# Sketched attention with a mixture of experts behind it on one core: a listed order for the first batch and a moved router placing

## The chip, the cores and the metric

One Trainium2 chip, one of its cores. The metric is device time in microseconds (us) of one execution of the kernel, median of several runs. The core has five engines that run beside each other[...]: TensorE (PE; its weight loads are shown as PEld), VectorE (DVE), ScalarE (ACT), GpSimd (POOL) and SyncE (SP), and 16 DMA engines that move data on request of SyncE, ScalarE or GpSimd.

## The reference

Inputs: q, k, v of shape (4, 4, 1088, 32), two sketches S1 and S2 of shape (8, 32), eight expert embeddings of 128, a temperature tau, w1 (8, 128, 1024) and w2 (8, 1024, 128), all float32. Output: (4352, 128).

```python
def phi(x):                      # 64 features of a row of 32
    a = np.einsum('rd,bhsd->bhsr', S1, x)
    b = np.einsum('rd,bhsd->bhsr', S2, x)
    return np.einsum('bhsi,bhsj->bhsij', a, b).reshape(*x.shape[:-1], r * r)
q_p, k_p = phi(q), phi(k)
kv = np.einsum('bhsf,bhsd->bhfd', k_p, v)
z = np.sum(k_p, axis=2)
x = num / den                    # q_p @ kv, over q_p @ z + 1e-6; heads side by side: (4352, 128)
logits = (x / |x|) @ (emb / |emb|).T / tau
expert_idx = np.argmax(logits, axis=1)
gate_w = softmax(logits)[expert_idx]
out[mask] = gate_w[mask, None] * (np.maximum(x[mask] @ w1[e], 0.0) @ w2[e])   # for each expert e
```

## The kernel before

The tokens are handled as two halves, m = 0 and m = 1 (two of the four batches each, 17 tiles of 128 tokens). The diff's words "first batch" and "second batch" mean these halves. Tiles go in groups of four (GROUPS: tiles 0 to 3, 4 to 7, 8 to 11, 12 to 15) and a single rest tile, called "r". For each group there are steps, small functions that issue instructions on several engines:

- `ktr`, `qtr`: four transposes on TensorE into a small PSUM bank ("t", two buffers) and a ScalarE copy (`turned`, L372 to L377). In the steps of the first half a 0 is added to the name (`ktr0 1`).
- `kab`, `qab`: the sketches of the group on TensorE (L392, L394), into a bank that the list names ("ab", "acc" or "t"). `kb`, `qb`: ScalarE copies of them (L400, or L405 where both factors are copied, `both_factors`). `kp`, `qp`: products of the two factors to 64 features (`features`, L410), on VectorE, for most key groups of the second half on GpSimd.
- For queries of the first half, features are made in turned form: `pairs` (32 matmuls into two pairs of big banks, L558), `sec` (ScalarE copies, L567), `prod` (VectorE products into the tile "held", L570).
- `kv` (L472): keys times values, summed over all tiles of the half in one bank ("acc"). `total`, `trkv`, `kvT`, `kve`, `kz`: the sum is copied and multiplied with the embeddings into the tile "kz".
- `trqp`, `qpT`: query features transposed (L588) and copied (L594 or L597). TWO_BANKS says for which groups the transposes go to the banks acc and ab instead of a pair of big banks. `nd` (L610): features times kz, into a pair of big banks. `x` (L623 to L630, VectorE): the attention rows (tile "xg") and their logits ("lg").
- The router (L680 on): `best`, `pick` (maximum and one-hot, VectorE), `place` (small matmuls that count each token's place within its expert, L702 to L706), `take`, `split`, `mark` (VectorE). `write` stores rows and logits to the DRAM tensor "rows" (SyncE, L732, L736). In the second half, the router works on two parts: tiles 0 to 7, then 8 to 16.
- The tables: the first half alone fills EARLY = 10 blocks of 128 tokens that belong to one expert each; `count`, `rest`, `find`, `exp0`, `sums` (L799, L801), `tokens` (L816) and `others` make the early table: which tokens lie in a block ("dst_i") and which expert it has ("exp_i"; exp_0 for the first block). A late table for the remaining blocks is made the same way when the second half has been routed, on ticks 13 to 17.

Then follow 36 blocks of the mixture of experts (MoE). For block i: `fetch` (an indirect gather of 128 rows on GpSimd's queue, L929), `turn` (a transpose into a bank "t", L935, and a copy xTb by ScalarE or VectorE, L937), `weights` (512 KB of w1 of the block's expert, issued by SyncE, which first reads the expert's number, L941, L946), `up` (16 matmuls into a pair of big banks, L983, and a ReLU on ScalarE, L991), `norm`, `inverse`, `shares`, `share` (the gate, ScalarE, GpSimd and VectorE), `down` (16 matmuls, L1019, alternately into acc and ab, then a scaled copy and an indirect scatter on GpSimd's queue, L1031).

What sets the order: every engine works off its instructions in the order in which they are emitted. `put_at(tick)(after, rank, f)` puts a step f on a tick with a rank; `emit` goes through the ticks, and within a tick by rank. Ticks below 4 hold the first half, tick 4 the long list ORDER, tick 10 + i block i of the MoE: second layer's address 29.9, up 30, turn of the next block 45, share 73, down of the block before 74, weights two blocks ahead 79. AFTER_UP stands at rank 30.5 and AFTER_TURN at rank 46 of tick 10. In the first half each step has a rank of its own in `keys`, `queries` and at the end (`put(0, 49.8, ab)` and so on), so that, within a stage, ScalarE copies `sec 0`, kT of the next group, `sec 1`, qT of the next group. The big banks are two pairs, handed out in turn: a new user of a pair waits until the one before it has been read.

In the list before, the step order behind the sums is: tokens, qp r, qp 3, qp 2 on VectorE, with the first gather (`fetch0`) after tokens. The router's first placing of the second half sits on tick 11 at rank 70.5, ahead of down(0) at 74, in a spare part of the big pair of `nd 1 3`.

Of the kernel before, what the change touches and what calls it, by code (L numbers as in the profile page):

```python
# [27 lines left out]
NC = S // HALF  # L28
# [9 lines left out]
SPAN = NC - 8  # L38
WIDE = SPAN + SPAN % 2
NEXT = 172  # L40
TWO_BANKS = (1, 2, 3)
NCP = 8 + WIDE
ROW = DM + E
COLS = D + 1 + E
# [21 lines left out]
def kernel(  # L66
# [284 lines left out]
    TABLE1 = 12  # L351


    ORDER = """
tremb; total0; ktr 1; trkv0; kvT0; kab 0 ab; kb 0; trqp0r; kve0; kab 1 acc; kz0; ktr 2; nd 0 0; kb 1; ktr 3;
kp 0; nd 0 1; kab 3 ab; kb 3; x 0 0; nd 0 2; kab 2 t; x 0 1; kp 1; x 0 2; kb 2; kp 3; kv 0; nd 0 3; ktr r;
qtr 0; kab r ab; kp 2; kb r; kv 1; x 0 3; qtr 1; qab 0 ab; best 0; qtr r; qb 0; kv 2; qtr 3; qp 0; place 0;
count; kv 3; kp r; take 0; kv r; total; qtr 2; qab 1 t; trqp 0; split 0; rest; trkv; qab 2 acc; find; kvT;
mark 01; mark 00; qab 3 ab; exp0; qb 1; qb 2; kve; qpT 0; qab r ab; qp 1; qb r; sums; tokens; qp r; qb 3; kz;
trqp 1; qp 3; fetch0; qp 2; qpT 1; nd 1 0; trqp 3; qpT 3; nd 1 1; fetch 1; turn 0; x 1 0; trqp 2; qpT 2;  # L360
norm 0
"""
    AFTER_UP = "others; x 1 1"
    AFTER_TURN = "nd 1 2; trqp r; qpT r; nd 1 3; x 1 2; x 1 3"
    steps = {}

    def turned(tiles, rest, n, tag):
# [66 lines left out]
        for bank in ("ab", "acc", "t"):  # L434
            steps[f"{name} {bank}"] = lambda bank=bank: f(bank)

    def keys(m, c0, c1, put=None):
        n = c1 - c0
        s = {}

        def tr():
            s["kT"] = turned(None if n == 1 else k_sb[m][:, :, c0:c0 + 4], k_rest[m], n, "kT")

        def ab(bank=None):
            s["ab"] = sketch(ab_bank(put.tick, n, 1) if put else ab_next("k", n, bank), s["kT"], n)

        both = m == 1
        by_pool = m == 1 and c0 > 0

        def b():  # L450
            if both:
                s["ab"] = both_factors(s["ab"], n)
                s["b"] = s["ab"][:, :, 1]
            else:
                s["b"] = second(s["ab"], n, "kb")

        def prod():
            s["kp"] = features(s["ab"], s["b"], n, "kp", nc.gpsimd if by_pool else nc.vector)

        def kv():  # L460

            if c0 == 0:
                acc[m] = ps_one("acc")[:, :8 * D].rearrange("p (i a n) -> p i a n", i=2, a=2)
            for c in range(c0, c1):
                rest = c == NC - 1
                for i in range(2) if rest else (c // NK,):
                    for p in range(2):
                        for u in range(2):
                            h = 2 * p + u
                            vo = v_rest[m][i][:, h] if rest else v_sb[m][:, h, c]  # L470
                            to_ones = (H - h) * D if rest else ((H - h) * 2 * NK - c) * D
                            nc.tensor.matmul(  # L472
                                acc[m][u * HALF:(u + 1) * HALF, i, p], s["kp"][:, c - c0, h],
                                bass.AP(tensor=vo.tensor, offset=vo.offset,
                                        ap=[list(vo.ap[0]), [to_ones, 2], [1, D]]),
                                start=p == 0 and c == 0, stop=rest, skip_group_check=True)

        def total():
            s["kv"] = work.tile([P, 2, 2, D], F32, tag="kv", bufs=1, name="kv")
            nc.scalar.copy(s["kv"], acc[m][:, :, :, :D])  # L480
            for u in range(2):
                r = slice(u * HALF, (u + 1) * HALF)
                nc.scalar.copy(kz[m][r, :, :, u, :D + 1], acc[m][r, :, :, :D + 1])

        def tr_kv():
            s["t"] = ps_small()[:, :P]
            nc.tensor.transpose(s["t"], s["kv"].rearrange("p i a d -> p (i a d)"), ident)

        def kvT():
            s["kvT"] = work.tile([P, P], F32, tag="kvT", bufs=1, name="kvT")  # L490
            nc.scalar.copy(s["kvT"], s["t"])

        def kve(stage):
            if stage == 0:
                s["kve"] = ps_small()[:, :P // 2]
                nc.tensor.matmul(s["kve"], s["kvT"], en_blk.rearrange("p a u e -> p (a u e)"), start=True, stop=True)
                return
            ps = s["kve"].rearrange("p (i a u e) -> p i a u e", i=2, a=2, u=2)
            for u in range(2):
                r = slice(u * HALF, (u + 1) * HALF)  # L500
                nc.scalar.copy(kz[m][r, :, :, u, D + 1:], ps[r, :, :, u])
        if m == 1:
            g = name_of(c0)
            steps.update({f"ktr {g}": tr, f"kb {g}": b, f"kp {g}": prod, f"kv {g}": kv})
            by_bank(f"kab {g}", ab)
            if n == 1:
                steps.update({"total": total, "trkv": tr_kv, "kvT": kvT, "kve": lambda: kve(0), "kz": lambda: kve(1)})
            return
        put(-1, 50.6 if n > 1 else 55.5, tr)
        put(0, 49.8, ab)  # L510
        put(0, 49.85, b)
        put(0, 53, prod)
        first = c0 >= NC - 5
        put(*((2, 51) if c0 == 0 else (1, 47) if first else (1, 55)), kv)
        if c1 == NC:
            steps.update({"total0": total, "trkv0": tr_kv, "kvT0": kvT, "kve0": lambda: kve(0), "kz0": lambda: kve(1)})

    xg, lg, spare, turned_q = {}, {}, {}, {}

    def queries(m, c0, c1, put=None):  # L520
        n = c1 - c0
        w = n * P
        s = {}
# [9 lines left out]
            s["qT"] = turned(None if n == 1 else q_sb[m][:, :, c0:c0 + 4], q_rest[m], n, "qT")  # L533

        def ab(bank=None):
            s["ab"] = sketch(ab_bank(put.tick, n, 0) if put else ab_next("q", n, bank), s["qT"], n)

        both = m == 1

        def b():  # L540
            if both:
# [91 lines left out]
        if n > 1:  # L633
            steps.update({f"nd {m} {step}": nd, f"x {m} {step}": x})
        if m == 0:
            put(-1, 53 if n > 1 else 55.6, tr)
            if n == 1:
                put(0, 50, ab)
                put(0, 50.5, b)
                put(0, 54, prod)  # L640
                steps.update({"trqp0r": tr_qp, "qpT0r": qpT})
            else:
                put(0, 50, pairs)
                for j in range(2):
                    put(0, 50.5 + 0.2 * j, lambda j=j: seconds(j))
                    put(0, 54, lambda j=j: prods(j))
        else:
            steps.update({f"qtr {step}": tr, f"qb {step}": b, f"qp {step}": prod,
                          f"trqp {step}": tr_qp, f"qpT {step}": qpT})
            by_bank(f"qab {step}", ab)  # L650
        if c1 == s1:

            bank = (lambda: spare[m]) if m == 0 or c1 < NC else (lambda: table_bank[0][:, 0])
            best, pick, place, take, split, mark, write = router(m, s0, s1, g, bank)

            if m == 0:
                steps.update({"best 0": best, "pick 0": pick, "place 0": place, "take 0": take, "split 0": split,
                              "mark 00": lambda: mark(0, NK), "mark 01": lambda: mark(NK, NC), "write 0": write})
            elif c1 < NC:
                at_rank = {best: (10, 72), pick: (10, 72), write: (10, 90), place: (11, 70.5),  # L660
                           take: (11, 71.2), split: (13, 76.5), mark: (14, 76)}
            else:
                at_rank = {best: (12, 31), pick: (12, 31), place: (13, 31), take: (13, 32), split: (13, 32),
                           write: (12, 90), mark: (16, 32)}
                put_at(13)(0, 30.9, lambda: table_bank.append(ps_big()))
# [381 lines left out]
    for i, group in enumerate(GROUPS):  # L1047
        for tiles in group:
            for m in range(NM):
                keys(m, *tiles, put_at(i) if m == 0 else None)  # L1050
                queries(m, *tiles, put_at(i) if m == 0 else None)
    put_at(-1)(0, 40, more_constants)
    put_at(-1)(0, 52.9, turn_sketches)
    put_at(1)(0, 55, iotas)
    put_at(2)(0, 60, norm_emb)
    put_at(3)(0, 51, scale_emb)
    put_at(3)(0, 52, steps["ktr 0"])
    put_at(1)(0, 91, lambda: clear(0))
    put_at(2)(0, 91, lambda: clear(1))

    count, rest, others = plan_early()
    find, high, low, sums, tokens, *_ = table(0, 1, lambda: early["key"])
# [12 lines left out]
    for i, name in enumerate(x.strip() for x in ORDER.split(";")):  # L1075
        put_at(4)(0, 47.2 + 0.01 * i, steps[name])
    for at_, names in ((30.5, AFTER_UP), (46, AFTER_TURN)):
        for i, name in enumerate(x.strip() for x in names.split(";")):
            put_at(first)(0, at_ + 0.01 * i, steps[name])
    put_at(first)(0, 32, lambda: weights(1))  # L1080

# [9 lines left out]
    put(3, 73.5, find)  # L1091
    put(3, 76, high)
    put(4, 74, low)
    put(5, 31, sums)
    put(5, 31.1, lambda: tokens(0, PAIRS))
    put(5, 45.1, first_rows)
    put(5, 75.1, halves)
    put(5, 75.2, lambda: tokens(PAIRS, LATE))
    known = table1 + 5 - first
    put(5, 31.2, lambda: [fetch(i) for i in range(EARLY, known + AHEAD + 1)])  # L1100

    def in_ticks(b0, b1, tick):
        for i in range(b0, b1 + 1):
# [79 lines left out]
```

## Time and profile before

| What | Value |
|---|---|
| median of 3 runs | 207.26 us (206.97 to 208.28) |
| the profiled execution | 206.99 us |
| its span (first to last instruction) | 205.2 us |
| TensorE busy, weight loads busy | 194.0 us, 183.3 us |
| VectorE, ScalarE, GpSimd busy | 87.8, 103.0, 106.8 us |
| first transpose of the MoE (L935) starts | 55.10 us |
| up(0), up(1), up(2) start | 56.30, 61.36, 67.27 us |
| DMA moved | 39.42 MB, 192 GB/s in the mean |

How to read it: times in a profile count from the start of the span. The page's slices show the busy share of 40 equal parts in tenths. A timeline line gives start, duration, engine, source line, operation, output tile <- input tiles, shape and count; brackets give the idle time of that engine just before and what ended it. A line of the waits reads: engine, tile and line that waited, <- who released it, then total us, times and the longest. "Issue" means that nothing in the profile explains the wait.

### The profile page before, as it was taken

Reading aid. Unit: us, or ns where it says so; the run is one execution under the profiler, and the core shown is the slowest. Engines: PE = TensorE matmul, PEld = TensorE weight load, DVE = VectorE, ACT = ScalarE, POOL = GpSimd, SP = SyncE. Lnnn points to the kernel's source line nnn. Section 1 sums busy time; section 2 is a strip of 40 time slices with the busy share of each in tenths; the row PEclk is TensorE's granted clock in tenths of the full one; section 3 lists DMA queues with packets and bytes.
Section 4 is the critical chain, followed back from the end, with each engine's and each line's share of the span. In section 5 each row is a group of like instructions: output and inputs, shape, how many; then the busy total and the mean of one; then the engine's idle time right before and its main releaser. Section 6 shows DMA issues by size and latency. Waiting matters only on the chain.

```text
span 205.2 us, 6948 instructions
## 1 busy us (share of the span) xinstructions
PE 194.0 (95%) x2586; PEld 183.3 (89%) x2586; DVE 87.8 (43%) x378; ACT 103.0 (50%) x294; POOL 106.8 (52%) x137
## 2 busy tenths in 40 slices
PE   7989998999897999999999999999999999998991
PEld 7658788798787999999999999999999999997891
DVE  6577847788948368931221312212122122122100
ACT  2656461436373546534654555546555465776330
POOL 4010035302743567666777767677676776753033
PEclk9999999999999999999999999999999999999999
DMA  4999899568354996645465665665656794592000
GB/s 132 334 274 315 179 311 292 165 221 248 70 216 136 318 341 175 184 155 154 146 199 177 165 210 156 181 196 154 210 161 176 229 313 152 200 268 114 3 26 24
DMA packets 28162, 39.42 MB, mean 192 GB/s; under 512 B 5738, under 2 KB 21366, under 8 KB 28130
## 3 DMA queue, kind: packets, MB, share of 16 engines
q1 hardware_dynamic: 25776, 34.23, 56.7%
q0 software_dynamic: 2304, 4.74, 7.6%
q8 instruction: 22, 0.36, 0.7%
q14 instruction: 10, 0.08, 0.1%
q10 hardware_dynamic: 50, 0.01, 0.0%
HBM read 34.37 MB, written 4.73 MB: 191 GB/s over the span
## 4 chain that ended last, share of the span: by engine, by line
PE 88%; DVE 3%; ACT 2%; DMA 2%; issue 2%; POOL 0%; POOLq 0%; DVEq 0%
PE ps_big L983 27%; PE ps_acc L1019 14%; PE ps_ab L1019 14%; PE ps_acc L472 4%; PE ps_big L610 4%; PE ps_big L988 4%; PE ps_t L375 4%; DMA xs<-rows,dst_i 2%; PE ps_t L935 2%; PE ps_big L558 2%; PE ps_acc L1022 2%; PE ps_ab L1022 2%; PE ps_t L801 2%; PE ps_acc L105 1%; PE ps_ab L394 1%
## 5 line engine op out<-in xcount | busy, mean ns | idle before, releaser
L983 PE MATMUL ps_big<-xTb,wb 128*128 128x128 f32 x512 | 62.8, 276 | 0.0
L1031 POOL DMA_INDIRECT out_dram<-y,dst_i x36 | 37.5, 1043 | 44.4 <-ACT sq L996 20.1
L983 PEld LDWEIGHTS ps_big<-xTb,wb 128*128 128x128 f32 x512 | 59.7, 192 | 0.5 <-issue 0.2
L991 ACT ACTIVATE hT<-ps_big 128x1024 f32<-128x1024 f32 x36 | 36.8, 1024 | 37.2 <-PE ps_big L983 36.4
L929 POOL DMA_INDIRECT xs<-rows,dst_i x36 | 37.6, 1043 | 18.9 <-DVE dst_i L816 10.9
L937 DVE COPY xTb<-ps_t 128x128 f32<-128x128 f32 x29 | 8.4, 291 | 61.9 <-PE ps_t L935 61.9
L1019 PE MATMUL ps_acc<-w_sb,hT 128*128 x256 | 31.3, 275 | 0.1
L1019 PE MATMUL ps_ab<-w_sb,hT 128*128 x256 | 31.2, 275 | 0.0
L1019 PEld LDWEIGHTS ps_acc<-w_sb,hT 128*128 128x128 f32 x256 | 29.9, 192 | 0.1
L1019 PEld LDWEIGHTS ps_ab<-w_sb,hT 128*128 128x128 f32 x256 | 29.9, 192 | 0.0
L997 POOL TENSOR_TENSOR norm<-norm,half_c 128x1 f32<-128x1 f32 x36 | 21.3, 595 | 3.6 <-ACT sq L996 3.0
L1010 DVE TENSOR_SCALAR gate<-gate 128x1 f32<-128x1 f32 x36 | 5.5, 152 | 22.1 <-ACT probs L1007 22.0
L1028 ACT ACTIVATE y<-ps_acc,gate 128x128 f32<-128x128 f32 x18 | 6.6, 367 | 14.3 <-PE ps_acc L1019 10.9
L410 POOL TENSOR_TENSOR kp<-both 128x1024 f32<-128x1024 f32 (+1 forms) x4 | 6.5, 1619 | 11.8 <-ACT both L405 10.8
L1028 ACT ACTIVATE y<-ps_ab,gate 128x128 f32<-128x128 f32 x17 | 6.2, 367 | 10.3 <-PE ps_ab L1019 8.7
L996 ACT ACTIVATE sq<-xs 128x128 f32<-128x128 f32 x36 | 10.9, 302 | 1.0 <-DMA xs<-rows,dst_i 0.9
L1007 ACT ACTIVATE probs<-xs,norm 128x8 f32<-128x8 f32 x36 | 10.6, 295 | 1.3 <-DVE norm L1001 1.3
L935 PE MATMUL ps_t<-ident,xs 128*128 128x128 f32 x36 | 10.2, 282 | 0.9 <-DMA xs<-rows,dst_i 0.9
L472 PE MATMUL ps_acc<-v,kp 128*64 128x64 f32 x256 | 9.4, 225 | 0.7 <-issue 0.5
L472 PEld LDWEIGHTS ps_acc<-v,kp 128*64 128x64 f32 x256 | 8.3, 138 | 1.6 <-issue 1.2
L377 ACT COPY kT<-ps_t 128x512 f32<-128x512 f32 (+1 forms) x10 | 5.2, 524 | 7.6 <-PE ps_t L372 3.8
L988 PE MATMUL ps_big<-xTb,wb 128*64 128x64 f32 x128 | 7.8, 223 | 0.0
(246 smaller groups left out, 291.2 us busy)
## 6 DMA issues: line engine op xcount, KB each, us to landing
wb<-in_moe_w_dram SPq DMA_DIRECT2D x36, 512.0 KB, 4.8
w_sb<-in_moe_w_dram SPq DMA_DIRECT2D x16, 256.0 KB, 4.8
rows<-xg SPq DMA_DIRECT2D x4, 544.0 KB
v<-in_v_dram SPq DMA_DIRECT2D x4, 512.0 KB
v<-in_moe_w_dram SPq DMA_DIRECT2D x4, 512.0 KB
k<-in_k_dram SPq DMA_DIRECT2D x3, 512.0 KB
q<-in_q_dram SPq DMA_DIRECT2D x3, 512.0 KB
xs<-rows,dst_i POOLq DMA_INDIRECT x36, 3.5
```

The costliest lines, as they stand in the source:

```text
L472: nc.tensor.matmul(acc[m][u * HALF:(u + 1) * HALF, i, p], s["kp"][:, c - c0, h], bass.AP(tensor=vo.tensor, offset=vo.offset, ap=[list(vo.a ...
L929: nc.gpsimd.indirect_dma_start(out=xs[i][:], out_offset=None, in_=rows[:2 * S if t == 0 else N + 1], in_offset=bass.IndirectOffsetOnAxis(a ...
L935: nc.tensor.transpose(ps[:, :P], xs[i][:, :DM], ident)
L983: nc.tensor.matmul(ps[:, u, j * P:(j + 1) * P], w[:, f * P:(f + 1) * P], x, start=True, stop=True)
L988: nc.tensor.matmul(ps[r, u, j * P + b * HALF:j * P + (b + 1) * HALF], wh[:, f * P + c * HALF:f * P + (c + 1) * HALF], x[:, b * HALF:(b + 1 ...
L991: nc.scalar.activation(hT[i], ps, ACT.Relu)
L996: nc.scalar.activation(sq, xs[i][:, :DM], ACT.Square, accum_out=norms[i])
L997: nc.gpsimd.tensor_tensor(out=norms[i], in0=norms[i], in1=half_c, op=ALU.pow)
L1007: nc.scalar.activation(p, xs[i][:, DM:], ACT.Exp, scale=norms.pop(i)[:, 0:1], accum_out=gate[i])
L1019: nc.tensor.matmul(ps, h[:, f * P:(f + 1) * P], ws[0][:, f], start=f == 0, stop=f == NF - 1)
L1028: nc.scalar.activation(y, ps, ACT.Copy, scale=gate.pop(i)[:, 0:1])
L1031: d = nc.gpsimd.indirect_dma_start(out=out[:, :], out_offset=bass.IndirectOffsetOnAxis(ap=dst_i[t][:, j:j + 1], axis=0), in_=y[:], in_offs ...
```

## The change

The first half's steps get names and an order of their own in a list HEAD, all at tick 0; ranks in `keys`, `queries` and at the end are gone. Within a stage, both `sec` copies now come before the copies of the next group, `kv0 1` comes behind the last `pairs`, and `iotas` and `scale emb` behind the rest tile. ORDER is rewritten; AFTER_UP becomes empty, with `others` and `x 1 1` moved into ORDER. Behind the sums VectorE's order is now qp 1, tokens, qp 3, qp 2, x 1 0, qp r, others, x 1 1; `fetch0` and the three further gathers stand next to each other. Query group 3 of the second half is no longer copied with both factors: its product reads one factor from PSUM. Group 1 leaves TWO_BANKS. The first placing of the second half takes a small bank and moves to tick 12 at 31.5, its take to 12 at 44, the write of the rows to tick 11 at 80. In the late table, sums and what follows (tokens, first_rows, two gathers) move from rank 31 to ranks 74.1 to 74.4 of tick 17, behind a down layer, and halves with its tokens to tick 18 at 46.

```diff
-TWO_BANKS = (1, 2, 3)
+TWO_BANKS = (2, 3)
...
+    HEAD = """
+constants; ktr0 0; sketches; qtr0 0; kab0 0; kb0 0; pairs 0; kp0 0; sec 0 0; sec 0 1; ktr0 1; qtr0 1; prod 0 0;
+prod 0 1; kab0 1; kb0 1; pairs 1; kp0 1; sec 1 0; sec 1 1; ktr0 2; qtr0 2; prod 1 0; prod 1 1; kab0 2; kb0 2; pairs 2;
+kp0 2; sec 2 0; sec 2 1; ktr0 3; qtr0 3; prod 2 0; prod 2 1; clear 0; kv0 0; kab0 3; kb0 3; pairs 3; kp0 3; sec 3 0;
+sec 3 1; ktr0 r; qtr0 r; prod 3 0; prod 3 1; kv0 1; norm emb; kab0 r; kb0 r; qab0 r; qb0 r; kp0 r; qp0 r; scale emb;
+iotas; clear 1; ktr 0; kv0 2; kv0 3; kv0 r
+"""
     ORDER = """
-tremb; total0; ktr 1; trkv0; kvT0; kab 0 ab; kb 0; trqp0r; kve0; kab 1 acc; kz0; ktr 2; nd 0 0; kb 1; ktr 3;
-kp 0; nd 0 1; kab 3 ab; kb 3; x 0 0; nd 0 2; kab 2 t; x 0 1; kp 1; x 0 2; kb 2; kp 3; kv 0; nd 0 3; ktr r;
-qtr 0; kab r ab; kp 2; kb r; kv 1; x 0 3; qtr 1; qab 0 ab; best 0; qtr r; qb 0; kv 2; qtr 3; qp 0; place 0;
-count; kv 3; kp r; take 0; kv r; total; qtr 2; qab 1 t; trqp 0; split 0; rest; trkv; qab 2 acc; find; kvT;
-mark 01; mark 00; qab 3 ab; exp0; qb 1; qb 2; kve; qpT 0; qab r ab; qp 1; qb r; sums; tokens; qp r; qb 3; kz;
-trqp 1; qp 3; fetch0; qp 2; qpT 1; nd 1 0; trqp 3; qpT 3; nd 1 1; fetch 1; turn 0; x 1 0; trqp 2; qpT 2;
-norm 0
+total0; ktr 1; ktr 3; tremb; kab 0 ab; trkv0; kvT0; kb 0; kab 1 acc; kp 0; ktr r; kve0; kz0; kb 1; kab 3 ab;
+ktr 2; nd 0 0; kab 2 t; kab r ab; nd 0 1; x 0 0; kb 2; x 0 1; trqp0r; nd 0 2; kb 3; kp 1; kb r; kv 0; x 0 2;
+nd 0 3; kp 2; x 0 3; qtr 1; kp 3; qtr 0; kv 2; qab 0 t; qb 0; qtr 3; kp r; best 0; kv 3; qtr r; qp 0; qtr 2;
+place 0; take 0; count; kv 1; kv r; trqp 0; total; split 0; qab 1 t; trkv; qab 3 ab; rest; mark 00; qb 1;
+qab r ab; mark 01; find; exp0; kvT; qab 2 acc; sums; kve; qb 2; qpT 0; qb 3; qb r; qp 1; tokens; qp 3; kz;
+trqp 1; nd 1 0; fetch0; fetch 1; qp 2; x 1 0; qp r; trqp 3; qpT 1; others; qpT 3; nd 1 1; x 1 1; norm 0; turn 0; trqp 2;
+qpT 2
 """
-    AFTER_UP = "others; x 1 1"
-    AFTER_TURN = "nd 1 2; trqp r; qpT r; nd 1 3; x 1 2; x 1 3"
+    AFTER_UP = ""
+    AFTER_TURN = "nd 1 2; x 1 2; trqp r; qpT r; nd 1 3; x 1 3"
...
-        put(-1, 50.6 if n > 1 else 55.5, tr)
-        put(0, 49.8, ab)
-        put(0, 49.85, b)
-        put(0, 53, prod)
-        first = c0 >= NC - 5
-        put(*((2, 51) if c0 == 0 else (1, 47) if first else (1, 55)), kv)
+        g = name_of(c0)
+        steps.update({f"ktr0 {g}": tr, f"kab0 {g}": ab, f"kb0 {g}": b, f"kp0 {g}": prod, f"kv0 {g}": kv})
...
-        both = m == 1
+        both = m == 1 and c0 != 12
...
-            bank = (lambda: spare[m]) if m == 0 or c1 < NC else (lambda: table_bank[0][:, 0])
+            bank = (lambda: spare[m]) if m == 0 else ps_small if c1 < NC else (lambda: table_bank[0][:, 0])
...
-                at_rank = {best: (10, 72), pick: (10, 72), write: (10, 90), place: (11, 70.5),
-                           take: (11, 71.2), split: (13, 76.5), mark: (14, 76)}
+                at_rank = {best: (10, 72), pick: (10, 72), write: (11, 80), place: (12, 31.5),
+                           take: (12, 44), split: (13, 76.5), mark: (14, 76)}
...
+    for i, name in enumerate(x.strip() for x in HEAD.split(";")):
+        put_at(0)(0, i, steps[name])
...
-    put(5, 31, sums)
-    put(5, 31.1, lambda: tokens(0, PAIRS))
-    put(5, 45.1, first_rows)
-    put(5, 75.1, halves)
-    put(5, 75.2, lambda: tokens(PAIRS, LATE))
+    put(5, 74.1, sums)
+    put(5, 74.2, lambda: tokens(0, PAIRS))
+    put(5, 74.4, first_rows)
+    put(6, 46, halves)
+    put(6, 46.1, lambda: tokens(PAIRS, LATE))
...
-    put(5, 31.2, lambda: [fetch(i) for i in range(EARLY, known + AHEAD + 1)])
+    put(5, 74.3, lambda: [fetch(i) for i in range(EARLY, known + AHEAD + 1)])
```

More of the change, by code (lines that the diff above doesn't have):

```diff
@@ L435, in by_bank, with keys @@
             steps[f"{name} {bank}"] = lambda bank=bank: f(bank)
-    def keys(m, c0, c1, put=None):
+    def keys(m, c0, c1, tick=None):
         n = c1 - c0
@@ L444, in ab @@
         def ab(bank=None):
-            s["ab"] = sketch(ab_bank(put.tick, n, 1) if put else ab_next("k", n, bank), s["kT"], n)
+            s["ab"] = sketch(ab_bank(tick, n, 1) if m == 0 else ab_next("k", n, bank), s["kT"], n)
         both = m == 1
@@ L518, with queries @@
     xg, lg, spare, turned_q = {}, {}, {}, {}
-    def queries(m, c0, c1, put=None):
+    def queries(m, c0, c1, tick=None):
         n = c1 - c0
@@ L535, in ab @@
         def ab(bank=None):
-            s["ab"] = sketch(ab_bank(put.tick, n, 0) if put else ab_next("q", n, bank), s["qT"], n)
-        both = m == 1
+            s["ab"] = sketch(ab_bank(tick, n, 0) if m == 0 else ab_next("q", n, bank), s["qT"], n)
+        both = m == 1 and c0 != 12
         def b():
@@ L635, in queries @@
         if m == 0:
-            put(-1, 53 if n > 1 else 55.6, tr)
+            steps[f"qtr0 {step}"] = tr
             if n == 1:
-                put(0, 50, ab)
-                put(0, 50.5, b)
-                put(0, 54, prod)
+                steps.update({"qab0 r": ab, "qb0 r": b, "qp0 r": prod})
                 steps.update({"trqp0r": tr_qp, "qpT0r": qpT})
             else:
-                put(0, 50, pairs)
+                steps[f"pairs {step}"] = pairs
                 for j in range(2):
-                    put(0, 50.5 + 0.2 * j, lambda j=j: seconds(j))
-                    put(0, 54, lambda j=j: prods(j))
+                    steps[f"sec {step} {j}"] = lambda j=j: seconds(j)
+                    steps[f"prod {step} {j}"] = lambda j=j: prods(j)
         else:
@@ L1049 @@
             for m in range(NM):
[L1050 to L1059, printed above, removed]
+                keys(m, *tiles, i)
+                queries(m, *tiles, i)
+    steps.update({"constants": more_constants, "sketches": turn_sketches, "iotas": iotas, "norm emb": norm_emb,
+                  "scale emb": scale_emb, "clear 0": lambda: clear(0), "clear 1": lambda: clear(1)})
+    for i, name in enumerate(x.strip() for x in HEAD.split(";")):
+        put_at(0)(0, i, steps[name])
     count, rest, others = plan_early()
@@ L1077 @@
     for at_, names in ((30.5, AFTER_UP), (46, AFTER_TURN)):
-        for i, name in enumerate(x.strip() for x in names.split(";")):
+        for i, name in enumerate(x.strip() for x in names.split(";") if x):
             put_at(first)(0, at_ + 0.01 * i, steps[name])
```

## The prediction

> **What bounds the kernel now.** I read the page first (busy time, the 40 slices), then TensorE's waits, the timelines of TensorE, VectorE and GpSimd from 5 to 100 us, the chain that ended last, and the DMA issues with their landings. From the page:
> ```profile
> PE 194.0 (95%) x2586; PEld 183.3 (89%) x2586; DVE 87.8 (43%) x378; ACT 103.0 (50%) x294; POOL 106.8 (52%) x137
> PE   7989998999897999999999999999999999998991
> ```
> TensorE is busy for 194.0 of 205.2 us, and nothing in the change takes matmuls away. All there is to win is the 11.2 us in which it waits. Its slices below 9 lie before 65 us and at the end. What it waited for before 80 us:
> ```profile
> PE ps_big L702 <- DVE oh L692: 1.2, 1, 1.2
> PE ps_acc L108 <- DVE mask L190: 1.1, 1, 1.1
> PE ps_t L935 <- DMA xs<-rows,dst_i: 0.9, 1, 0.9
> PE ps_big L558 <- ACT qT L377: 0.6, 2, 0.3
> PE ps_ab L394 <- ACT kT L377: 0.5, 2, 0.3
> PE ps_acc L472 <- issue: 0.5, 1, 0.5
> PE ps_t L375 <- ACT kT L377: 0.4, 1, 0.4
> ```
> Without the start (L108) that is 4.1 us: the ceiling of the gain. The end (1.5 us of issue in L1022, 4 us of tail) is not touched. The two largest waits, and the work that each hangs on, in the timelines (TensorE, VectorE, GpSimd):
> ```profile
> 55.10 0.33 PE L935 MATMUL ps_t<-ident,xs 128*128 128x128 f32 x1 [0.94 <-DMA xs<-rows,dst_i]
> 64.74 0.19 PE L702 MATMUL ps_big<-oh,before 128*128 128x64 bf16 x1 [1.22 <-DVE oh L692]
> ...
> 49.66 0.18 DVE L816 TENSOR_REDUCE dst_i<-ps_t 128x10 int32<-128x20 f32 x1 [0.69 <-PE ps_t L801]
> 49.75 2.69 DVE L410 TENSOR_TENSOR qp<-both 128x256 f32<-128x256 f32 x3
> 65.16 0.27 DVE L937 COPY xTb<-ps_t 128x128 f32<-128x128 f32 x1
> ...
> 50.13 2.24 POOL L929 DMA_INDIRECT xs<-rows,dst_i  x1 [10.91 <-DVE dst_i L816]
> 52.68 0.97 POOL L929 DMA_INDIRECT xs<-rows,dst_i  x1 [0.30 <-issue]
> ```
> To be seen: the first transpose of the MoE (L935) waits for the first gather. That gather takes 2.24 us on GpSimd, the next 0.97, and the long one lies under three VectorE products (49.75 to 52.44). And the placing (L702) stands in TensorE's queue ahead of the first down layer, waiting for VectorE's one-hot, with ready work behind it.
>
> **What the Trainium skill says.** SBUF — State Buffer, Who interferes with whom: a VectorE instruction with two SBUF inputs contends with a GpSimd instruction that reads SBUF, as an exclusive lock; PSUM inputs don't. The trace agrees: 2.24 us beside products of two SBUF inputs, 0.94 to 0.99 for the next four gathers. (The page infers that descriptor generation escapes such an instruction; this trace says it doesn't.) TensorE: Matmul & The Clock Gate, Architectural detail: VectorE's and ScalarE's queues are strict FIFO; the trace agrees, the copy at 65.16 stands behind the router's reductions though its transpose ended at 63.5. DMA: Bandwidth & Descriptors, Anatomy of one DMA: about 2 us of a GpSimd DMA are fixed, most of it after the last byte; here 2.73 us pass from the gather's end on GpSimd (52.37) to the matmul (55.10).
>
> **The change part by part.** Times "new" are worked out from before's durations. TensorE steps: four transposes 0.59, one sketch 0.61, kv of four tiles 1.08, trqp 0.95, nd 1.29 (1.60 for the one with five tiles), up or down layer 1.79, turn 0.11. VectorE: product 1.2, x 1.8 (2.1 for five tiles), best with pick 2.4.
>
> *First batch (HEAD).* ScalarE's copies start 0.48 to 0.55 apart. The kT copy becomes third of its stage instead of second: it ends at 10.06, not 9.58, so the sketch runs 10.1 to 10.7 and the pairs start at 10.71 instead of 10.62 (+0.09). In return both feature copies come first, the second held product starts 0.5 earlier, and the two banks are free: the pairs that now take 1.34 should take 1.12 like the first (7.25). That is -0.13 a stage, 0.4 in three stages; I take -0.3, since kv0 1 no longer fills the last one. Moved past others: kv0 1 behind the last pairs (two steps still cover the banks), the iotas (2.5 us of VectorE, three GpSimd instructions) from 14.4 to behind scale emb, about 23.5 to 26.0; the embedding's placing is then done at 26.5, and kve0 asks for it at 27.2. Hidden, 0.7 to spare. Bounds: 0 to -1.1 (all four waits gone).
>
> *ORDER up to the table.* ktr r moves from 36.5 to about 27, where other steps stand between it and the next user of its bank: the 0.35 wait goes. Nothing in the edit explains the 0.52 of issue in kv 0; I keep it (0 to -0.5). nd 0 3 has 0.3 more TensorE work ahead (ktr r, kab r, less the gain above): its end goes from 36.5 to 36.8. From there VectorE is the path: x 0 3 and best to 41.1, qp 0 to 42.2, a wait for the placing (42.8), take, count, split 44.0, rest 45.2, marks 46.6, find 47.55, exp0 47.9, qp 1 49.05. TensorE reaches the sums at 48.41 - 0.3 - 0.35 - 0.17 (kve goes behind) = 47.6, as find is ready; they take 1.15, to 48.75. The tokens then follow qp 1 without the 0.69 of idleness, at 49.06 instead of 49.66: -0.6.
>
> *qp 3 from PSUM (`c0 != 12`), qp r behind x 1 0.* The product next to the tokens has only one SBUF input. By the lock, the first gather takes 0.97 as its neighbours do. Issue 49.53 (0.47 after the tokens, as now), end 50.5, landed 53.23. Without the effect (bound 0) 54.5. Behind it fetch 1 meets qp 2, which has two SBUF inputs: up to 1.2 later, and needed only after up(0). TensorE meanwhile: trqp 1 from 49.05 (behind qp 1) to 50.0, nd 1 0 51.3, trqp 3 52.25, nd 1 1 53.55. So turn 0 starts at 53.55, bound by TensorE: 55.10 - 53.55 = -1.55 (bounds -0.6 and -1.9). The product itself costs the same: 1.23 from PSUM (10.77), 1.20 from SBUF. trqp 1 in a big pair of banks: one copy of 1.02 instead of two of 0.58, hidden under nd 1 0.
>
> *Others and x 1 1 ahead of up(0).* VectorE: qp 3 50.45, qp 2 51.65, x 1 0 53.4, qp r 53.8, others 54.3, x 1 1 56.0. nd 1 2, which needs that bank, comes at 56.65. The expert list (written in others) lets SyncE issue weights(1) 0.56 later, 54.85; landings take 3.9 to 4.8, to 58.7 to 59.65, and up(1) comes at 59.9. Hidden, with 0.3 to spare at worst.
>
> *Placing in a small bank, after up(2).* From nd 1 3's end to up(2) is now 61.48 to 67.27, 5.79 us. Freed of the placing, TensorE has up(1), turn, down(0) = 3.7. But xT of block 2 still comes from VectorE behind x 1 3 and best: 61.48 to 65.43, 3.95. So up(2) follows nd 1 3 after 4.0: -1.8. The 12 small matmuls are paid after up(2), 0.35 (the second placing, 72.57 to 72.92). Net -1.45. Take moves behind the second best on VectorE; the small bank is wanted again by turn(4), 3 us later. The rows' write moves behind weights(3) on SyncE: weights(3), now issued at 64.82 because the write waits for VectorE, goes at about 56.5. That earns nothing by itself, but landed at 69.2 it would cost 1.4 us once up(3) comes at 67.8.
>
> *Late sums behind a down layer.* 2.06 us of TensorE move behind down(6), the sum the same: 0. Gathers 10 and 11 go behind that block's scatter and are issued about 0.45 after the sums; turn(10) comes 5.6 us after the sums (up, turn, down, up), and landings take 3.4 in the median: 1.7 to spare. At the longest landing (5.2, the held one) 0.05 would be lost.
>
> Sum: -1.55 - 1.45 = -3.0 on a span of 205.2, so 202.2; the profiled execution took 206.99, so 204.0. The median of the runs shown is 207.26, 0.27 more: I say 204.3. A measurement here can tell about 1% (2.1 us) from no change.
>
> **The rivals.**
> - *The gather stays slow* (the lock isn't what stretched it, or POOL meets qp 2 first): turn 0 at 54.5, -0.6 - 1.45: 205.2. Against it: four undisturbed neighbours under 1 us.
> - *VectorE becomes the bound after nd 1 3*: x 1 2 and x 1 3 slip, because qp 2 and qp r must wait for gathers in a row (1 us each), and xT of block 2 returns TensorE's 1.2 us wait under another name. Gain 1 us or less: 206.3. For it: VectorE's step there already exceeds TensorE's by 0.25.
> - *Slower*: weights(1) arrives late. The expert list is now behind qp 2, x 1 0 and qp r on VectorE; after 54.6 each microsecond delays up(1). up(2) is later than today's 67.27 - 0.35 once up(1) starts after 63.2, so once the list is written after 57.8, which is 3.5 us late; two held products explain 2. At 60, the time is 209.5.
> - *More*: every wait above goes, -4.1: 203.1.
> - *That HEAD does not reorder*: it does, every step is named in it; its effect is small in all cases.
>
> **How the numbers follow.** Forecast 0.57 (203.6 to 205.1), slow gather 0.14 (205.2, half of it below the 1% mark of 205.2), VectorE bound 0.13 (205.5 to 207), slower 0.10 (above 209), more 0.06. Faster by over 1%: 0.57 + 0.07 + 0.06 = 0.70; within 1%: 0.07 + 0.13 = 0.20; slower: 0.10. Range for 8 in 10: 203.3 to 206.6.
>
> **What would show it.** Right: pairs of 1.1 us each; the tokens near 49.1; a first gather near 1 us; no wait at L935; up(2) about 4 us after nd 1 3's end; the placing without a wait. Wrong: a gather still over 2 us, a wait at L983 for weights or for VectorE's xTb copy, or L801 waiting for find by more than a few tenths.

## The result and the profile after

| | before | after |
|---|---|---|
| median | 207.26 us (206.95 to 208.93, 6 runs) | 205.05 us (204.43 to 205.92, 6 runs) |
| ratio, 95% interval | | 0.9874 [0.9837, 0.9910] |
| profiled execution, its span | 206.99, 205.2 us | 204.43, 202.6 us |

Ratios, here and below, leave out executions more than 1.5% above the fastest of their kernel, so they need not be the quotient of the medians. The kernel is 2.2 us faster; the forecast was 204.3 us, or 3.0 less. The page of the kernel after, TensorE's slices and the engines' busy times:

```profile
PE 192.7 (95%) x2586; PEld 182.7 (90%) x2586; DVE 87.6 (43%) x378; ACT 102.4 (51%) x293; POOL 107.0 (53%) x137
PE   7889999999799999999999999999999999999991
```

The work is the same (2586 matmuls). The three slices from 51 to 67 us, 8 9 7 before, are now 7 9 9: one dip has gone and one has stayed, for another reason. TensorE's waits before 80 us, after (engine, tile and line, releaser, total, times, longest):

```profile
PE ps_big L984 <- ACT xTb L938: 1.4, 1, 1.4
PE ps_ab L401 <- ACT kT L384: 1.3, 2, 0.7
PE ps_acc L108 <- DVE mask L190: 1.1, 1, 1.1
PE ps_acc L479 <- issue: 0.5, 1, 0.5
PE ps_big L824 <- DVE lt L712: 0.4, 1, 0.4
PE ps_t L399 <- ACT kb L407: 0.3, 1, 0.3
PE ps_big L984 <- DVE norm L1001: 0.2, 1, 0.2
```

The two waits that the change aimed at, 1.2 us at the placing (now L703) and 0.9 at the first transpose (now L936), are off the list. The 1.4 at the top is new. The timelines of TensorE, VectorE and GpSimd, after:

```profile
52.66 0.33 PE L936 MATMUL ps_t<-ident,xs 128*128 128x128 f32 x1
55.26 2.05 PE L984 MATMUL ps_big<-xTb,wb 128*128 128x128 f32 x16 [1.40 <-ACT xTb L938]
66.59 0.19 PE L703 MATMUL ps_t<-oh,before 128*128 128x64 bf16 x1
...
48.01 0.18 DVE L817 TENSOR_REDUCE dst_i<-ps_t 128x10 int32<-128x20 f32 x1 [0.20 <-PE ps_t L802]
48.56 1.23 DVE L417 TENSOR_TENSOR qp<-ps_ab,qb 128x1024 f32<-128x1024 f32 x1 [0.37 <-ACT both L412]
49.70 1.22 DVE L417 TENSOR_TENSOR qp<-both 128x1024 f32<-128x1024 f32 x1
...
48.49 1.20 POOL L930 DMA_INDIRECT xs<-rows,dst_i  x1 [11.27 <-DVE dst_i L817]
50.00 1.75 POOL L930 DMA_INDIRECT xs<-rows,dst_i  x1 [0.30 <-issue]
```

The first gather takes 1.20 us instead of 2.24, turn 0 starts 2.44 us earlier and without a wait, and the placing runs without a wait behind up(2). But from turn 0 to up(0), 1.03 us before, now pass 2.60. I cut each span at five marks, each the start of a TensorE step, so that the differences add up to that of the spans (by these marks up(0) and up(2) of before start at 56.13 and 67.11, a little earlier than the 56.30 and 67.27 listed ahead):

| from, to | before | after | difference | forecast |
|---|---|---|---|---|
| start, first pairs | 7.25 | 6.80 | -0.45 | 0 |
| first pairs, turn 0 | 47.85 | 45.86 | -1.99 | -1.55 |
| turn 0, up(0) | 1.03 | 2.60 | +1.57 | 0 |
| up(0), up(3) | 14.66 | 13.56 | -1.10 | -1.45 |
| up(3), up(30) | 102.55 | 102.60 | +0.05 | 0 |
| up(30), end | 31.87 | 31.23 | -0.64 | 0 |
| span | 205.2 | 202.6 | -2.56 | -3.0 |

The third row was the open question, and whether the first and last rows belong to the change at all.

### The profile page after: what moved, and what is told of

Read it like the earlier page. It is cut to its first block, busy times and chain, and to the rows that moved or that the text cites. A ratio compares the mean times of both kernels' runs of the same rounds, so it can differ in the third digit from the quotient of the medians.

```text
span 202.6 us, 6949 instructions
## 1 busy us (share of the span) xinstructions
PE 192.7 (95%) x2586; PEld 182.7 (90%) x2586; DVE 87.6 (43%) x378; ACT 102.4 (51%) x293; POOL 107.0 (53%) x137
## 4 chain that ended last, share of the span: by engine, by line
PE 90%; DVE 4%; ACT 2%; issue 1%; DMA 1%; POOL 0%; POOLq 0%; DVEq 0%
PE ps_big L984 28%; PE ps_ab L1020 14%; PE ps_acc L1020 13%; PE ps_big L613 5%; PE ps_acc L479 4%; PE ps_big L989 4%; PE ps_t L382 3%; PE ps_t L936 2%; PE ps_ab L401 2%; PE ps_big L561 2%; PE ps_acc L1023 2%; PE ps_ab L1023 2%; PE ps_t L802 2%; ACT qpT L570 1%; PE ps_ab L591 1%
## 5 line engine op out<-in xcount | busy, mean ns | idle before, releaser
L936 PE MATMUL ps_t<-ident,xs 128*128 128x128 f32 x36 | 10.2, 282 | 0.2 <-issue 0.2
L479 PE MATMUL ps_acc<-v,kp 128*64 128x64 f32 x256 | 9.2, 225 | 0.5 <-issue 0.5
L319 POOL TENSOR_TENSOR emb_ss<-emb_ss,half_c 8x1 f32<-8x1 f32 x1 | 0.6, 576 | 17.1 <-ACT emb_sq L318 17.1
L479 PEld LDWEIGHTS ps_acc<-v,kp 128*64 128x64 f32 x256 | 8.2, 138 | 1.5 <-issue 1.5
L989 PE MATMUL ps_big<-xTb,wb 128*64 128x64 f32 x128 | 8.3, 224 | 0.3 <-issue 0.2
```

Source lines behind the costliest of these rows:

```text
L479: nc.tensor.matmul(acc[m][u * HALF:(u + 1) * HALF, i, p], s["kp"][:, c - c0, h], bass.AP(tensor=vo.tensor, offset=vo.offset, ap=[list(vo.a ...
L936: nc.tensor.transpose(ps[:, :P], xs[i][:, :DM], ident)
L989: nc.tensor.matmul(ps[r, u, j * P + b * HALF:j * P + (b + 1) * HALF], wh[:, f * P + c * HALF:f * P + (c + 1) * HALF], x[:, b * HALF:(b + 1 ...
```

## The experiments

They ran in three sets, each on one chip that also ran the kernel before (median 207.55 us with e1, e2, e3, p1; 204.97 with p2, e4, e5, e6; 205.4 with g0, g1, g2), so ratios are compared across sets, not times. What lengthens the third row I call "the late release"; e1 shows why.

**e1: the changed kernel again, unchanged.**

> The changed kernel once more, unchanged. In its first profile TensorE waited 1.40 us ahead of up(0): the last matmul of nd 1 1 ended at 52.73, yet the releases of nd 1 1, of turn 0 and of the transposes behind it came only at 54.88 to 56.42, where releases elsewhere come 0.02 us after the end. Theory A (a hiccup of that one execution): the wait is gone here, up(0) starts near 53.9, and the span is about 1.4 us shorter than 202.6, unless another hiccup falls elsewhere. Theory B (it belongs to this order of steps): the wait of 1 us or more stands again in front of up(0). Also open: TensorE's first pairs started 0.45 us earlier than in the kernel before, with the same instructions ahead of them; if that is chance, it varies here too. Ratio to before 0.987.

205.18 us, 0.9890 [0.9830, 0.9951]. The wait came again: turn 0 at 52.69, up(0) at 55.31. So it is no accident of one execution. What happens is in the timelines of the kernel after. TensorE's transposes (L591) and ScalarE's and VectorE's next instructions:

```profile
52.82 0.60 PE L591 MATMUL ps_acc<-ident,qp 128*128 128x128 f32 x4
53.26 0.60 PE L591 MATMUL ps_ab<-ident,qp 128*128 128x128 f32 x4
...
54.94 0.27 ACT L938 COPY xTb<-ps_t 128x128 f32<-128x128 f32 x1 [2.48 <-PE ps_ab L591]
55.10 0.59 ACT L600 COPY qpT<-ps_acc 128x512 f32<-128x512 f32 x1
56.44 0.58 ACT L600 COPY qpT<-ps_ab 128x512 f32<-128x512 f32 x1 [0.75 <-remote]
...
54.90 0.17 DVE L626 TENSOR_SCALAR rc<-ps_big 128x16 f32<-128x16 f32 x1 [1.59 <-PE ps_ab L591]
```

The transpose that ScalarE's copy needs (L936) ended at 52.98, yet the copy started at 54.94, and VectorE, which needs `nd 1 1` (ended 52.73), started at 54.90. Both engines stood idle until then. The trace's records of TensorE's semaphore show the releases of four matmul groups (`nd 1 1`, turn 0 and the two halves of the transposes) at 54.88, 54.91, 54.97 and 56.42; in g1 below, the same releases follow the ends by 0.02 us. The end of a matmul is modelled in a profile, so a late release and a late end look alike here. It isn't the only place in this trace: an up layer that ended at 99.63 was released at 100.31, but there TensorE had other work and lost nothing.

**e2: query product 3 from SBUF again.**

```
-        both = m == 1 and c0 != 12
+        both = m == 1
```

> The changed kernel with one part undone: query group 3 is again copied with both factors, so the product next to the tokens has two SBUF inputs. Theory of the port lock: the first gather takes over 2 us again instead of 1.20, and turn 0 waits for it about 0.7 us (tokens 48.0, landing about 5 us later at 53.2, TensorE ready at 52.66). Rival (the gather was long only because it was the first, or because of the weights' load): the gather stays near 1.2 us. Time: 0.3 to 0.7 us more than the changed kernel under the lock, none under the rival.

205.54 us, 0.9909 [0.9874, 0.9945]: not told apart from e1. The expectation for the gather was wrong: it took 1.20 us, as with the product from PSUM. GpSimd and VectorE of e2:

```profile
48.95 1.20 POOL L930 DMA_INDIRECT xs<-rows,dst_i  x1 [11.28 <-DVE dst_i L817]
50.46 1.74 POOL L930 DMA_INDIRECT xs<-rows,dst_i  x1 [0.30 <-issue]
...
49.01 2.36 DVE L417 TENSOR_TENSOR qp<-both 128x1024 f32<-128x1024 f32 x2 [0.36 <-ACT both L412]
```

The gather starts at 48.95, 0.06 us before the two-input product, and isn't held; the next one starts at 50.46 inside the second product and takes 1.74. With qp r moved away from behind the tokens, product 3 has to wait 0.36 us for ScalarE, and the gather goes first. In this order PSUM isn't what saves it. Taken alone, a first gather of 1.20 us is what the rival expected; but the next one, with 0.91 us of the product left, takes 0.79 longer than the usual 0.95, which goes with the lock.

**e3: the placing ahead of down(0) again, in the small bank.**

```
-... write: (11, 80), place: (12, 31.5), take: (12, 44), ...
+... write: (11, 80), place: (11, 70.5), take: (11, 71.2), ...
```

> The changed kernel with the first placing put back ahead of down(0) (tick 11, rank 70.5, take 71.2), still in a small bank. My account: TensorE waits again about 1.2 us for the one-hot ahead of down(0), and from the end of nd 1 3 to up(2) it takes 5.8 us instead of 4.0; placing paid earlier gives 0.3 back: 1.4 to 1.5 us slower than the changed kernel. Rival (the xTb copy of block 2 or weights(2) sets up(2) anyway): less than 0.5 us.

206.14 us, 0.9918 [0.9894, 0.9943], 0.6 us over e1 by the ratios, where 1.4 to 1.5 were expected; the intervals overlap, so the time neither shows the cost of the early place nor rules it out. The profiled execution took 208.81 us, well over the median, so only its structure is read: the wait is back as before, and from the end of `nd 1 3` to up(2) pass 5.64 us instead of 4.04. TensorE's waits of e3:

```profile
PE ps_t L703 <- DVE oh L693: 1.2, 1, 1.2
```

**p1: in the kernel before, the placing alone** (small bank, placing after up(2), take and write moved).

> The kernel before with one part of the change alone: first placing of the second half in a small bank on tick 12 at 31.5, take at 12/44, the rows' write at 11/80. My account: 1.4 us of the gain come from this part, at any place of the rest: ratio to before about 0.993, the 1.22 us wait at the placing gone, up(2) about 4 us after the end of nd 1 3. Rival (the gain needs the rest of the change, because up(2) then waits for the next weights): under 0.5 us.

206.97 us, 0.9958 [0.9933, 0.9983]: 0.9 us less by the ratio. From up(0) to up(3) 13.57 us, as in the kernel after (13.56; before 14.66). The late release is here too, in the old order of steps, and it costs TensorE time twice: ahead of up(0), and again behind the late sums, where up waits 0.74 us (the view names VectorE's L1000):

```profile
PE ps_big L983 <- ACT xTb L937: 1.3, 1, 1.3
...
93.85 0.27 PE L935 MATMUL ps_t<-ident,xs 128*128 128x128 f32 x1
96.30 0.29 DVE L937 COPY xTb<-ps_t 128x128 f32<-128x128 f32 x1 [4.06 <-PE ps_ab L1019]
```

This transpose ended at 94.12, its release is recorded at 96.28, and VectorE, idle since 92.2, copied at 96.30. So up(3) to up(30) takes 103.54 us here, against 102.56 in before and 102.52 in g2 below, which has the same placing.

**p2: in the kernel before, product 3 from PSUM and qp r behind x 1 0, alone.**

```
-        both = m == 1
+        both = m == 1 and c0 != 12
-... sums; tokens; qp r; qb 3; kz; ...  turn 0; x 1 0; trqp 2; qpT 2;
+... sums; tokens; qb 3; kz; ...  turn 0; x 1 0; qp r; trqp 2; qpT 2;
```

> The kernel before with one part of the change alone: query group 3's product reads its first factor from PSUM, and the rest tile's product (qp r) moves from right behind the tokens to behind x 1 0. Port lock: the first gather shortens from 2.24 to about 1.2 us and turn 0's 0.94 us wait goes; TensorE then has its own work up to turn 0, so up(0) comes 0.9 us earlier, and from there the old wait at the placing keeps its 1.2 us: ratio 0.995 to 0.996. Rival (no lock): no change within 0.3 us.

206.17 us, 1.0033 [0.9994, 1.0072]: nothing gained. The gather fell to 1.20 us, but turn 0 came at 55.63. The timelines of TensorE, VectorE and GpSimd of p2:

```profile
49.92 1.06 PE L588 MATMUL ps_ab<-ident,qp 128*128 128x128 f32 x4 [1.01 <-DVE qp L410]
...
48.56 1.22 DVE L410 TENSOR_TENSOR qp<-ps_ab,qb 128x1024 f32<-128x1024 f32 x1
51.01 1.23 DVE L410 TENSOR_TENSOR qp<-both 128x1024 f32<-128x1024 f32 x1 [1.24 <-PE ps_ab L588]
...
48.94 1.20 POOL L929 DMA_INDIRECT xs<-rows,dst_i  x1 [10.89 <-DVE dst_i L816]
```

The product that reads PSUM holds its bank until it ends (49.78). trqp 1, by TWO_BANKS, wants bank ab for its second half and waits 1.01 us; qp 2 waits for trqp 1, and the rest follows. The wait for the gather was replaced by a wait for a bank.

**e4: the late sums where they were.**

```
-    put(5, 74.1, sums)
+    put(5, 31, sums)
... (tokens, first_rows, halves and the fetches likewise)
```

> The changed kernel with the late table's sums, tokens, two gathers, first_rows and halves put back to ranks 31 to 75 of tick 17. My account: 0, within 0.3 us, since the 2 us of sums stand in TensorE's queue either way and nothing waits. Rival (the sums' old place stalled something that the page doesn't show): up to 0.5 us slower.

202.62 us, 0.9877 [0.9832, 0.9923]; up(3) to up(30) takes 102.72 instead of 102.60 us. The moved sums are worth 0.1 us at most. (In this profile the first gather's data came about 2 us late and turn 0 waited 1.5 us; in no other run.)

**e5: in HEAD, kT copied second again**, `sec 0 0; ktr0 1; sec 0 1; qtr0 1` and so on in three stages.

> The changed kernel with one part undone: in the first half's stages 0 to 2, ScalarE copies sec 0, kT, sec 1, qT again instead of sec 0, sec 1, kT, qT. My account: 0.1 us a stage slower, 0.3 in all: the pairs take 1.34 instead of 1.12 again, the sketch's wait for kT shrinks from 0.67 to 0.3. Rival (a stage is bound by the chain of four ScalarE copies and one group of pairs, whatever their order): 0.

202.61 us, 0.9905 [0.9865, 0.9945]. TensorE's waits of e5:

```profile
PE ps_big L561 <- ACT qT L384: 0.6, 2, 0.3
PE ps_ab L401 <- ACT kT L384: 0.5, 2, 0.3
```

The total is about that of the kernel after (1.1 against 1.3), only split between pairs and sketch, but two of the pairs also take 1.34 us again instead of 1.12. From the first pairs to the end of the last, 11.97 us against 11.59. By the end of `nd 0 3` 29.02 against 29.17, as if the 0.4 were gone; but in the kernel after this holds a wait of 0.49 us at `kv 0` (L479, "issue") that e5 doesn't have, and that varies from 0 to 1.0 us between profiles of the same list. Without it the kernel after, e1, e2, e3 and g1 take 28.7 us, e6, which doesn't have it either, 28.4, and e5 29.0. So kT second costs 0.3 to 0.6 us, as expected; the medians are too coarse to show it.

**e6: norm 0 behind qpT 2 at the end of the list.**

> The changed kernel with norm 0 put back behind qpT 2, so that ScalarE copies xT of block 0 first and squares afterwards. If the wait ahead of up(0) in the changed kernel's profile has to do with the square in front of that copy, it goes here and up(0) comes 1.4 us earlier; if it is a hiccup of one execution, this kernel differs by less than 0.3 us from the changed one in time.

202.19 us, 0.9871 [0.9835, 0.9907], the ratio of the whole change: norm's place doesn't matter. No late release in e4, e5 or e6: turn 0 to up(0) takes 1.03 to 1.04 us in each, so neither the new order nor, in e4 and e5, norm 0's place brings it by itself.

**g0, g1, g2: the kernel before, the kernel after, and the second half's edits alone**, on a third chip. g2 is p1 and p2 together with one more line, the bank:

```
-TWO_BANKS = (1, 2, 3)
+TWO_BANKS = (2, 3)
```

> The kernel before, unchanged, for its profile. Theory A (late releases of TensorE's semaphores between nd 1 1 and up(0) go with the chip or the execution, not with the order of the steps): from turn 0 to up(0) the time is either 1.0 to 1.2 us in both this kernel and the changed one of this call, or 2.3 to 2.7 us in both. Theory B (the order of the change brings them): 1.0 to 1.2 us here and 2.3 to 2.7 us in the changed kernel. Both: up(0) to up(1) 5.2 us, the first gather 2.2 us on GpSimd.

> The changed kernel, unchanged. Theory A: as the kernel before of this call does. Theory B: 2.3 to 2.7 us from turn 0 to up(0). If there is no late release here, the span is 3.0 to 3.7 us shorter than that of the kernel before, else 2.2 to 2.6 us; the median is 0.984 to 0.990 of the kernel before.

> The kernel before with the second half's three edits alone (placing in a small bank after up(2) with its take and write, query product 3 from PSUM with the rest tile's product behind x 1 0, trqp 1 no longer in the two banks), but the first half's steps and most of the long list as before. Theory 1 (these three are the gain, the two lists bring little): the first gather takes 1.2 us, turn 0 starts at 53.6 to 54.2 without a wait for VectorE's product at L588, up(2) comes 4.0 us after the end of nd 1 3, the ratio is 0.985 to 0.991 as for the whole change. Theory 2 (the lists bring most of what precedes turn 0, because they shorten the way to the tokens): turn 0 at 54.5 or later, the ratio 0.992 to 0.998, as for the placing alone.

| | g0 | g1 | g2 |
|---|---|---|---|
| median, us | 204.89 | 202.69 | 202.55 |
| ratio to before | 0.9993 [0.9959, 1.0027] | 0.9869 [0.9811, 0.9927] | 0.9875 [0.9816, 0.9934] |
| start, first pairs | 6.61 | 7.18 | 7.02 |
| first pairs, turn 0 | 47.75 | 46.56 | 46.68 |
| turn 0, up(0) | 1.04 | 1.04 | 1.04 |
| up(0), up(3) | 14.63 | 13.48 | 13.48 |
| up(3), up(30) | 102.56 | 102.60 | 102.52 |
| up(30), end | 30.79 | 30.83 | 30.14 |
| span | 203.4 | 201.7 | 200.9 |

No late release in either order, as Theory A of g0 allows. My span for g1 (3.0 to 3.7 us shorter) was missed, it is 1.7 shorter: g1 happened to start 0.57 later than g0, where its predecessor had started 0.45 earlier. The medians differ by 2.7 us. Theory 1 of g2 holds in the time: the three edits give the ratio of the whole change. But each interval reaches 1.2 us to both sides, so a microsecond from the two lists would not show; from the first pairs to turn 0, the profiles with both lists take 45.10 to 46.56 us (e4 with its late gather aside), g2 46.68. The edits also don't add: 0.9958 times 1.0033 is 0.9991, together with the bank it is 0.9875.

TensorE in the stretches of the change, g0 (columns: stretch, its length, busy us and count of PE, PEld, DVE, ACT, POOL, granted clock, DMA share, GB/s):

```profile
47.00:54.00 7.00, 6.64 (x117) 5.84 (x112) 6.16 (x17) 4.06 (x10) 3.77 (x3) 1.00 0.56 154
54.00:70.00 16.00, 14.37 (x177) 13.60 (x178) 10.28 (x44) 7.96 (x25) 8.12 (x11) 1.00 0.63 201
70.00:172.00 102.00, 102.00 (x946) 101.84 (x946) 32.49 (x175) 53.87 (x167) 71.99 (x82) 1.00 0.64 196
```

The same of g1:

```profile
47.00:54.00 7.00, 7.00 (x134) 6.41 (x131) 6.30 (x15) 4.30 (x12) 3.81 (x3) 1.00 0.53 159
54.00:70.00 16.00, 15.81 (x193) 15.08 (x192) 10.58 (x48) 8.21 (x26) 8.71 (x12) 1.00 0.72 237
70.00:172.00 102.00, 102.00 (x972) 101.68 (x973) 32.69 (x176) 53.86 (x167) 72.13 (x82) 1.00 0.63 191
```

Between 47 and 70 us TensorE's idle time falls from 2.0 to 0.2 us (23 less 6.64 and 14.37; less 7.00 and 15.81): this is the change. From 70 to 172 us TensorE is never idle in either kernel, so nothing that only reorders work there can pay.

## Why the prediction was right, step by step

Direction, mechanism and range were right. That the first pair of spans came within 0.5 us of the forecast difference is in part luck: a term forecast at nothing cost 1.57 us, and two that belong to no edit gave back 1.09. Seen against the steps as forecast:

- **HEAD.** Right: the pairs take 1.12 us each, the waits for kT rose from 0.3 to 0.66 each, and against the same list the order of the copies is worth 0.3 to 0.6 us (e5), forecast 0.3. Old against new it can't be read off: from the first pairs to the end of `nd 0 3` the five profiles with the old head have 28.48 to 29.41 us, the eight with the new one (e5's among them) 28.41 to 29.70. ORDER moved work ahead of `nd 0 3`, as the forecast counted, and the wait at `kv 0`, kept at 0.52 in the forecast, varies by up to 1.0 us.
- **ORDER.** nd 0 3 to tokens: forecast 12.3 (from 36.8 to 49.06), 13.1 before; measured 12.04 to 12.48 in the changed orders, 13.11 to 13.14 in all five old ones. Right. The forecast's 0.3 later end of nd 0 3 wasn't there. The tokens, forecast at 49.06, came at 49.10 in g1 and at 48.01 in the result's profile.
- **First gather.** Forecast 0.97, measured 1.20, against 2.24: right in size. The reason given, a PSUM operand, was half right. Without qp r behind the tokens the gather starts first, and then even a product with two SBUF inputs doesn't hold it (e2); p2 shows that a PSUM product doesn't either. The second gather met qp 2 and took 0.8 longer, hidden as said.
- **Turn 0 bound by TensorE.** Right: no wait at L936, forecast 53.55, measured 53.74 in g1 (52.66 in the result's profile, whose tokens came 1.1 us earlier). From first pairs to turn 0 the gain is 1.2 us (g1 against g0) to 2.0 (after against before), forecast 1.55.
- **Turn 0 to up(0).** "As before" failed in the result's own profile: +1.57 us, the term that hid most of the extra gain ahead of it. The prediction named a wait at the up layer for VectorE's xTb copy as a sign of being wrong; a wait for ScalarE's came, but not from a busy engine: the releases were late. On the two other chips it was absent, with the new order in four profiles and the old one, or nearly, in three (p2, g0, g2).
- **Placing.** nd 1 3's end to up(2): forecast 4.0, measured 4.04 (5.68 before); up(2) to up(3) +0.44, forecast +0.35. The sum from up(0) to up(3) is -1.10 and -1.15, not -1.45: I had started from 5.79 us where the same measure gives 5.68, and a wait of 0.2 for VectorE stays ahead of up(2) (put down to L1001, right behind the copy of xT). VectorE is the bound there, by 0.2 us; the rival that feared for a microsecond didn't come about.
- **Weights.** The rival that ends slower stayed away: no wait of an up layer for a load, with weights(1) issued at 54.07 and needed at 60.58.
- **Late sums and gathers 10, 11.** Forecast 0, measured 0 to -0.1 (e4).
- **Which edits carry it.** The forecast put 1.45 on the placing and 1.55 on the rest. p1 gives -0.9 and p2 +0.7 us by the ratios, together with the bank -2.6 (g2). The bank choice, for which I wrote only "hidden", is what p2 lacks: its wait of 1.01 us at L588 isn't in g2. That the second edit pays with the bank alone is read from these two profiles; no run had the two without the placing.

The medians gained 2.2 and 2.7 us, where the sum said 3.0. The terms of the change itself, without start, end and late release, add up to -3.0 in the first pair of profiles (-1.99 - 1.10 + 0.05) and to -2.3 in g1 against g0. The 0.45 at the start and the 0.64 at the end of the first pair belong to no step of the change: the same instructions stand ahead of the first pairs in both kernels, whose start ranges from 6.61 to 7.45 over all profiles without regard to the order, and up(30) to the end from 30.1 to 31.9. Part of the latter is "issue" time in the last blocks; before's profile had one such wait of 1.5 us in L1022, g0's had 0.4.

What stays open: what makes TensorE's releases late. They were late, at several places, in the kernel after, e1, e2, e3 and p1, the last four on one chip. These five traces hold 133 to 136 records of TensorE's releases where the other eight hold 187 or 188, so part is missing. In the other eight (before, p2, e4, e5, e6, g0, g1, g2) no release came over 0.07 us after its end. That it goes with the chip is likely, not shown: the unchanged kernel wasn't profiled on that chip, and whether the missing records have to do with it isn't known. The kernel before is slower there too (207.55 us against 204.97 and 205.4). In the kernel after and in e1 the profiled execution wasn't longer than the others (204.43 of 204.43 to 205.92; 204.78 of 204.05 to 205.99), and the ratios (0.987 and 0.989 with it, 0.987 without) don't tell whether it lengthens every run there.

## What to carry to other kernels

Before moving an operand from SBUF to PSUM to spare another engine, write down who gets that bank next: here the lock went and a bank wait of the same size came (p2), which isn't there when the next user has another bank (g2). Moving the other product away from behind the tokens gave the short gather with both factors in SBUF too (e2); whether that would have done without PSUM and bank in the old order, no run tested. A wait at the head of an in-order queue that only needs later data is removed by moving the waiting step behind work that is ready, as the placing was; the gain is what the next-latest input allows, here VectorE's chain 0.2 us behind. Compare two profiles mark to mark, not by their spans: between executions of the same kernel the start differed here by up to 0.6 us and the end by up to 1.1 (before and g0), half of the effect. And when a mark hides a wait that varies by itself, as the one at `kv 0` does, take it out before reading a difference of 0.4.

## What the runs showed of the hardware

**A gather issued while a product with two SBUF inputs (128x1024) runs is held until about 0.12 us before that product's end**, and then takes its usual time; one that starts first (e2), or beside a product with a PSUM input (p2, g2), isn't held. The usual time is 1.20 us for the first gather and 0.95 for the next. In each of the thirteen profiles one gather met such a product, and each time the excess over the usual time is 0.10 to 0.13 us less than the rest of the product at its start; for example before, first gather: rest 1.17, excess 1.04; after, second: 0.92 and 0.80; p2, third: 0.52 and 0.39; g2, second: 0.45 and 0.34. The Trainium skill (SBUF — State Buffer, Who interferes with whom) describes this exclusive lock, but infers that descriptor generation escapes it. A gather isn't free of it here; it also reads its indices (`dst_i`) from SBUF, and no run tells which part of it was held.

**TensorE's releases came up to 2.8 us after the matmul's end as the profile has it** (p1, `nd 1 1`: 53.86 to 56.69), at several places in five of thirteen profiles; in the other eight, never more than 0.07 us.

**The wait from the gather's end on GpSimd to its first reader** was 2.73 us in before, 2.53 in p1 and 2.50 in g0, where the reader waited for it (the view of g0 names VectorE, but the last landing is recorded at 54.31, just before turn 0 at 54.36). That is in line with the fixed part of about 2 us that the Trainium skill gives (DMA: Bandwidth & Descriptors, Anatomy of one DMA). It isn't constant: the last landing on record came 1.6 to 2.3 us after the gather's end in the other profiles, and 4.5 us after it in e4.
